# A loop over jobs of two matmul stages: the order of twelve matmuls, and the next expert's scales and first weight piece in branches

## The chip, the core and the metric

The kernel runs on one core of a Trainium2 chip. The metric is the device time of one execution in microseconds, lower is better. The engines of a core run side by side, each in the order of its own program: TensorE (PE, with its weight loads as PEld), VectorE (DVE), ScalarE (ACT), GpSimd (POOL) and SyncE (SP), which issues most DMAs. They wait for one another through semaphores.

## What is computed

An RWKV-like attention over 4 x 768 tokens gives rows of 384 numbers; each row then goes through one of eight experts. The change touches the experts alone. Of the reference:

```python
def _moe_ref(x, modality_id, w_gate, modality_bias, w1, w2):   # x: 3072 x 384, E = 8, F = 1024
    ...
    for e in range(E):
        mask = e_idx == e
        ...
        h = np.maximum(x[mask] @ w1[e], 0.0)
        out[mask] = gate_w[mask, None] * (h @ w2[e])
```

## The kernel before

Attention and routing fill about the first 200 us; there the tokens are written to `rows` in memory, sorted by expert, and nine tiles of 128 tokens of the fullest expert are worked on beside the attention. What is left is a table of jobs, made on the chip: each job is 128 tokens of one expert, and a job's code (a number) says what has to be done about weights beside it. The first job stands ahead of the loop (`up("a", ...)`, `job_terms`), the others are the turns of `tc.For_i` in `run`; in this run the loop makes 16 turns.

A matrix product in float32 is made of three float16 products. Weights `raw` are split into a high part `whi` (`wide`, ScalarE: scaled and rounded) and a low part `wlo` (`fine`, VectorE: what the rounding left), in six pieces: 0 to 2 are the first matrix, 3 to 5 the second. The scale `ws` comes from the sums of squares of `raw` (`norm`, ScalarE, into `ssq`), summed over partitions by a small matmul `pw` with ones on TensorE and turned into a power of two by four small VectorE operations (`scales_`). Tokens `xT` have both parts too.

One job on TensorE:

- `up`: the first matrix, in groups of 4, 2 and 2 blocks of 128 hidden units (`raise_`, 36, 18 and 18 matmuls of 128 columns). After each group ScalarE takes the relu's high part `hh` (`relu_high`) and VectorE its low part `hl` (`relu_low`). `beside()` after a group runs other work: behind group 0 `change(code, 5)` and `due`, behind group 1 `scales("2")`.
- `job_terms`: the second matrix, 20 of its 24 matmuls of 384 columns into `po`; a term is `hh` or `hl` of one block f with `whi` or `wlo`. Its order before: `hh whi` 0-3, `hh wlo` 0-3, `hh whi` 4-7, `hl whi` 0-3, `hh wlo` 4-7.
- `rest_terms`: `hl whi` 4-7, at the start of the next turn. Then `put`: ScalarE multiplies `po` by the tokens' factor `fac`, and POOL stores the rows by an indirect DMA at `ids`.

Around it in a turn: SP fetches the next job's tokens (`turn`, into `xn` and `mn`); VectorE copies them into `xT` and `m2` when `up` has read them (`take_in`). `due` makes `fac` and `ids` of the job from `m2`. Where the code says so, blocks of `tc.If` are entered: `square` (the next expert's sums of squares, two pieces a bit), `first_half` (the job ahead of a change of expert: pieces 0 to 2 are split into `whi` and `wlo` after the job's own use of them), `change` (the first job of a new expert: pieces 3, 4 and 5) and `next_load` (SP: the load of the weights after those). ScalarE and VectorE meet such a block in each job; where it isn't entered they compare, jump, and bring their semaphore to the count that the block would have left, for which they first wait for their own last operation.

The order of instructions inside a turn is that of the code (`manual_schedule`) on DVE, ACT, PE and SP.

Of the kernel before, what the change touches and what calls it, by code (L numbers as in the profile page):

```python
# [18 lines left out]
P = 128  # L19
# [18 lines left out]
NQ = 6  # L38
# [26 lines left out]
class _Kernel:  # L65
# [942 lines left out]
    def up(self, key, beside=lambda: None, late=False):  # L1008
        sizes = [4, 2, 2]
        for g, fb in enumerate(sizes):  # L1010
            f0 = sum(sizes[:g])
            ph = self.ps_a.tile([P, 512], F32, tag="big", name=f"ph{key}{g}")
            self.raise_(ph, f0, fb)
            self.relu_high(ph, f0, fb)
            low = lambda ph=ph, f0=f0, fb=fb: self.relu_low(ph, f0, fb)
            low()
            beside()

# [54 lines left out]
    def job_terms(self, po):  # L1073

        half = FB // 2
        for lo in (0, half):
            for f in range(lo, lo + half):
                self.term(po, 0, self.hh, self.whi, f, first=f == 0)
            if lo:
                for f in range(half):  # L1080
                    self.term(po, 0, self.hl, self.whi, f)
            for f in range(lo, lo + half):
                self.term(po, 0, self.hh, self.wlo, f)

    def rest_terms(self, po):
        for f in range(FB // 2, FB):
# [12 lines left out]
    def run(self):  # L1099
        nc, tc, m = self.nc, self.tc, self.m  # L1100
# [307 lines left out]
        xn = m.tile([P, 2 * DC, P], F16, name="xn", bufs=1)  # L1408
        mn = m.tile([P, 2, 4], I16, name="mn", bufs=1)
        self.turn(0, self.at(ROW, slice(1, 2), E * CAP, SP), mn, xn)  # L1410
        take_in = lambda: (nc.vector.tensor_copy(self.xT[:, :, :P], xn), nc.vector.tensor_copy(m2[:, 0, :], mn[:, 0, :]))
        take_in()
        po = self.ps_y.tile([P, 512], F32, tag="y", name="po")
        self.job_terms(po)
# [6 lines left out]
        def square(code):  # L1421
            with tc.If(code % (1 << pairs) > 0):
                for n in range(pairs):
                    with tc.If(code % (2 << n) >= 1 << n):
                        norms(2 * n, 2 * n + 1)

        def first_half(code):
            with tc.If(code % (2 << pairs) >= 1 << pairs):  # L1428
                for q in range(NQ // 2):
                    self.split(q, 2 if q == 0 else 1)  # L1430

        def change(code, q):
            with tc.If(code >= 1 << STEPS):  # L1433
                self.split(q)
                if q == NQ // 2:
                    self.undo()

        def next_load():
            more = self.at(MORE, i, 2 * E - 1, SP)
# [3 lines left out]
        with tc.For_i(1, nj, 1, iteration_sync="reg_based") as i, tc.manual_schedule(engines={getattr(mybir.EngineType, e) for e in MS[:4]}):  # L1443
# [4 lines left out]
            square(code)  # L1448
            self.put(po, 0, "b")
            change(code, 4)  # L1450
            beside = iter([lambda: (change(code, 5), self.due(m2)), lambda: self.scales("2")])
            self.up("b", lambda: next(beside, lambda: None)(), True)
            next_load()
            take_in()
            self.job_terms(po)
            first_half(code)
        self.rest_terms(po)
# [44 lines left out]
```

## Time and profile before

| | us |
|---|---|
| median of 3 runs | 353.18 |
| lowest and highest | 351.89, 359.52 |
| the profiled execution | 351.33 |
| its span, first to last instruction | 349.4 |

| engine | busy us | share of the span | instructions |
|---|---|---|---|
| PE | 328.5 | 94% | 5555 |
| PEld | 265.8 | 76% | 5555 |
| DVE | 221.4 | 63% | 740 |
| ACT | 179.1 | 51% | 476 |
| POOL | 156.6 | 45% | 230 |

The granted TensorE clock is 0.989 of full over the span. The loop's turns begin at 210.12 us and end near 342.4; the rest of the span behind it is the last job's rest and its store. Busy shares over the whole span say little of the loop, so the rows below are taken from its stretches. In a timeline, matmuls that follow each other in one group are merged into one row with their count, and the number of the row is from the first's start to the last's modelled end; where a wait lies inside such a row it is longer than its like.

### The profile page before, as it was taken

The numbers are of one execution on the slowest core, as the hardware profiler recorded it, in microseconds if no ns is written. First come the engines' busy times: TensorE is split into PE (matmuls) and PEld (weight loads), VectorE is DVE, ScalarE is ACT, GpSimd is POOL, SyncE is SP. The second block draws the span as 40 slices with busy tenths as digits, with TensorE's granted clock in tenths as the row PEclk, the third lists the DMA queues.
The fourth block names the chain that finished last, engine by engine and source line by source line (L and its number), as shares of the span: only waits on it lengthen the run. The fifth ranks groups of instructions, "written<-read, shape, count | busy, mean of one in ns | idle before, by whom it ended". The sixth has DMA issues, their size and how long they took to land. (4 is left out here: it accounts for less than half of the span.)

```text
span 349.4 us, 15387 instructions
## 1 busy us (share of the span) xinstructions
PE 328.5 (94%) x5555; PEld 265.8 (76%) x5555; DVE 221.4 (63%) x740; ACT 179.1 (51%) x476; POOL 156.6 (45%) x230
## 2 busy tenths in 40 slices
PE   8999998868999999999998999998999999999992
PEld 3788997757878888897887777776777777777771
DVE  8878899798997877684768633368333332333950
ACT  7777874966866748556532222265222224542920
POOL 8988869765737856242268311113112110221311
PEclk9999999989999999999999999999999999999997
DMA  6785868996649999492336531226821121112120
GB/s 190 222 166 159 179 164 253 328 257 146 162 114 212 244 290 216 99 197 72 70 115 202 170 103 35 58 50 220 192 67 45 45 62 29 45 45 68 23 58 5
DMA packets 56798, 46.96 MB, mean 134 GB/s; under 512 B 42920, under 2 KB 50359, under 8 KB 56496
## 3 DMA queue, kind: packets, MB, share of 16 engines
q1 hardware_dynamic: 53552, 36.86, 44.5%
q0 software_dynamic: 3200, 9.47, 7.7%
q8 instruction: 31, 0.51, 0.6%
q14 instruction: 15, 0.12, 0.1%
HBM read 26.03 MB, written 11.83 MB: 108 GB/s over the span
## 5 line engine op out<-in xcount | busy, mean ns | idle before, releaser
L997 PEld LDWEIGHTS <-whi 128*128 128x128 f16 x1248 | 72.4, 98 | 3.9 <-issue 1.1
L1006 DVE SCALAR_TENSOR_TENSOR hl<-phb,hh 128x256 f16<-128x256 f32 (+1 forms) x48 | 24.6, 512 | 69.3 <-ACTq L1433 47.8
L1060 PEld LDWEIGHTS <-hh 128*128 128x128 f16 x416 | 37.9, 98 | 31.9 <-ACTq L1428 3.8
L997 PE MATMUL phb<-mxT,whi 128*128 128x128 f16 x768 | 50.8, 219 | 0.0
L410 ACT ACTIVATE dv<-kv,d 128x48 f32<-128x48 f32 x172 | 43.0, 324 | 3.0 <-issue 2.0
L1001 ACT ACTIVATE hh<-phb 128x256 f16<-128x256 f32 (+1 forms) x48 | 21.4, 454 | 40.7 <-PE phb L997 21.4
L997 PEld LDWEIGHTS <-wlo 128*128 128x128 f16 x624 | 37.7, 98 | 0.2 <-DVE wlo L943 0.2
L371 POOL TENSOR_TENSOR rk<-rc,kc 112x512 f32<-112x512 f32 x20 | 25.7, 1286 | 24.1 <-DVE ebx L309 10.9
L966 POOL TENSOR_TENSOR seenb<-otb,putb 128x1 int32<-128x1 int32 x16 | 4.5, 282 | 64.8 <-ACTq L1433 51.6
L430 DVE TENSOR_TENSOR at<-psc,mask 128x512 f32<-128x512 f32 x48 | 31.7, 682 | 2.2 <-PE psc L424 2.1
L359 POOL TENSOR_TENSOR rc<-ud,powr 112x512 f32<-112x512 f32 (+1 forms) x25 | 31.2, 1252 | 2.7 <-DMA ud<-in_pd 1.9
L1060 PE MATMUL po<-whi,hh 128*128 128x384 f16 x136 | 29.7, 327 | 1.7 <-ACT whi L938 1.1
L1060 PEld LDWEIGHTS <-hl 128*128 128x128 f16 x208 | 19.5, 98 | 15.0 <-issue 3.0
L665 POOL DMA_INDIRECT rows<-row,posi x24 | 24.9, 1039 | 10.4 <-DVE pr L742 3.6
L1060 PE MATMUL po<-whi,hl 128*128 128x384 f16 x136 | 28.0, 326 | 1.5 <-DVE hl L1006 0.7
L997 PE MATMUL phb<-mxT,wlo 128*128 128x128 f16 x384 | 29.3, 219 | 0.0
L424 PE MATMUL psc<-rc,kc 64*64 64x128 f32 (+1 forms) x768 | 28.6, 286 | 0.6 <-issue 0.4
L1060 PE MATMUL po<-wlo,hh 128*128 128x384 f16 x136 | 27.7, 326 | 0.0
L957 ACT ACTIVATE otb<-po,fac 128x384 f32<-128x384 f32 x16 | 9.3, 579 | 35.6 <-PE phb L997 28.5
L997 PE MATMUL phs<-mxT,whi 128*128 128x128 f16 x432 | 27.2, 219 | 0.0
L424 PEld LDWEIGHTS psc<-rc,kc 64*64 64x64 f32 (+1 forms) x768 | 22.1, 138 | 6.5 <-issue 2.9
L943 DVE SCALAR_TENSOR_TENSOR wlo<-raw,ws,whi 128x1024 f16<-128x1024 f32 (+1 forms) x20 | 25.4, 1299 | 1.9 <-ACT whi L938 1.2
(272 smaller groups left out, 641.2 us busy)
## 6 DMA issues: line engine op xcount, KB each, us to landing
kv<-in_pt SPq DMA_DIRECT2D x21, 384.0 KB
raw<-in_w SPq DMA_DIRECT2D x12, 512.0 KB
ud<-in_pd SPq DMA_DIRECT2D x12, 384.0 KB
raw<-in_w SPq DMA_DIRECT2D x2, 1536.0 KB, 7.3
ud<-in_pd SPq DMA_DIRECT2D x12, 192.0 KB
rows<-pad SPq DMA_DIRECT2D x10, 193.0 KB
kv<-in_pt SPq DMA_DIRECT2D x6, 192.0 KB
rows<-row,posi POOLq DMA_INDIRECT x24
```

What stands on the lines that cost most here:

```text
L359: nc.gpsimd.tensor_mul(u["rc"][:TOP, s], u["rT"][:TOP, s], self.powr[:TOP, s])
L371: nc.gpsimd.tensor_mul(u["rk"][:TOP], u["rc"][:TOP], u["kc"][:TOP])
L410: nc.scalar.activation(u["dv"][:, sl], u["v"][:, sl], AF.Copy, scale=u["d"][:, h : h + 1])
L424: nc.tensor.matmul(u["ps"][j][s, pr * P : (pr + 1) * P], u["kc"][r, pr, s], u["rc"][r, pr, :], start=True, stop=True)
L430: nc.vector.tensor_mul(u["at"][:, j * NPR : (j + 1) * NPR, :], u["ps"][j].rearrange("p (q t) -> p q t", q=NPR), self.mask.unsqueeze(1).to_ ...
L665: i = nc.gpsimd.indirect_dma_start(out=self.rows, out_offset=bass.IndirectOffsetOnAxis(ap=u["posi"][:, b : b + 1], axis=0), in_=u["row"][: ...
L943: self.nc.vector.scalar_tensor_tensor(self.wlo[:, sl], self.raw[:, sl], sc, self.whi[:, sl], ALU.mult, ALU.subtract)
L957: self.nc.scalar.activation(ot, po[:, :DM], AF.Copy, scale=gf[:, t : t + 1])
L997: self.nc.tensor.matmul(ph[:, q * P : (q + 1) * P], w[:, c0 : c0 + P], self.xT[:, xq, t * P : (t + 1) * P], start=i == q == 0, stop=i == l ...
L1001: self.nc.scalar.activation(self.hh[:, f0 : f0 + fb, t * P : (t + 1) * P], p3, AF.Relu)
L1006: self.nc.vector.scalar_tensor_tensor(self.hl[:, f0 : f0 + fb, r], p3, 0.0, self.hh[:, f0 : f0 + fb, r], ALU.max, ALU.subtract)
L1060: self.nc.tensor.matmul(po[:, :DM], h[:, f, t * P : (t + 1) * P], w[:, c0 : c0 + DM], start=first, stop=last)
```

## The change

Four things, all in the table's jobs:

- `job_terms` takes `hl whi` 0-3 ahead of `hh whi` 4-7.
- The scales are no longer made in each job behind group 1. The small matmul `pw` stands behind group 0 of each job, and the four VectorE operations are in a branch that is entered only in the job ahead of a change (`weigh`), together with the two halves of `wide` for piece 0. This stands ahead of `relu_low` of group 0.
- Behind `relu_low` of group 0 comes `either`: a branch for the jobs of a change or ahead of one, holding `change(code, 5)` and, in a further branch, the two halves of `fine` for piece 0. `first_half` keeps pieces 1 and 2.
- `due` moves from behind group 0 to `take_in`, between its two copies.

```diff
@@ -1013,6 +1013,8 @@
             self.raise_(ph, f0, fb)
             self.relu_high(ph, f0, fb)
             low = lambda ph=ph, f0=f0, fb=fb: self.relu_low(ph, f0, fb)
+            if late and g == 0:
+                beside()
             low()
             beside()
 
@@ -1074,13 +1076,9 @@
 
         half = FB // 2
         for lo in (0, half):
-            for f in range(lo, lo + half):
-                self.term(po, 0, self.hh, self.whi, f, first=f == 0)
-            if lo:
-                for f in range(half):
-                    self.term(po, 0, self.hl, self.whi, f)
-            for f in range(lo, lo + half):
-                self.term(po, 0, self.hh, self.wlo, f)
+            for h, w in ((self.hh, self.whi), (self.hh, self.wlo), (self.hl, self.whi))[: 2 if lo else 3]:
+                for f in range(lo, lo + half):
+                    self.term(po, 0, h, w, f, first=f == 0 and h is self.hh and w is self.whi)
 
     def rest_terms(self, po):
         for f in range(FB // 2, FB):
@@ -1408,7 +1406,7 @@
         xn = m.tile([P, 2 * DC, P], F16, name="xn", bufs=1)
         mn = m.tile([P, 2, 4], I16, name="mn", bufs=1)
         self.turn(0, self.at(ROW, slice(1, 2), E * CAP, SP), mn, xn)
-        take_in = lambda: (nc.vector.tensor_copy(self.xT[:, :, :P], xn), nc.vector.tensor_copy(m2[:, 0, :], mn[:, 0, :]))
+        take_in = lambda between=lambda: None: (nc.vector.tensor_copy(self.xT[:, :, :P], xn), between(), nc.vector.tensor_copy(m2[:, 0, :], mn[:, 0, :]))
         take_in()
         po = self.ps_y.tile([P, 512], F32, tag="y", name="po")
         self.job_terms(po)
@@ -1424,16 +1422,34 @@
                     with tc.If(code % (2 << n) >= 1 << n):
                         norms(2 * n, 2 * n + 1)
 
+        near = lambda code: tc.If(code % (2 << pairs) >= 1 << pairs)
+
         def first_half(code):
-            with tc.If(code % (2 << pairs) >= 1 << pairs):
-                for q in range(NQ // 2):
-                    self.split(q, 2 if q == 0 else 1)
+            with near(code):
+                for q in range(1, NQ // 2):
+                    self.split(q)
 
         def change(code, q):
             with tc.If(code >= 1 << STEPS):
                 self.split(q)
                 if q == NQ // 2:
                     self.undo()
+
+        def weigh(code):
+            steps = self.scales_("2")
+            next(steps)
+            with near(code):
+                for _ in steps:
+                    pass
+                for part in range(2):
+                    self.wide(0, part, 2)
+
+        def either(code):
+            with tc.If(code >= 1 << pairs):
+                change(code, NQ - 1)
+                with near(code):
+                    for part in range(2):
+                        self.fine(0, part, 2)
 
         def next_load():
             more = self.at(MORE, i, 2 * E - 1, SP)
@@ -1448,10 +1464,10 @@
             square(code)
             self.put(po, 0, "b")
             change(code, 4)
-            beside = iter([lambda: (change(code, 5), self.due(m2)), lambda: self.scales("2")])
+            beside = iter([lambda: weigh(code), lambda: either(code)])
             self.up("b", lambda: next(beside, lambda: None)(), True)
             next_load()
-            take_in()
+            take_in(lambda: self.due(m2))
             self.job_terms(po)
             first_half(code)
         self.rest_terms(po)
```

The first place is on TensorE, between the first and the second half of `job_terms` in a turn of the loop. Before (`REGISTER_ALU` works out the count that is waited for):

```order
L1060 LDWEIGHTS hh
L1060 MATMUL po<-wlo,hh 128x384
L1060 REGISTER_ALU
L1060 LDWEIGHTS hh [waits Activation_I-4853_own]
L1060 MATMUL po<-whi,hh 128x384
L1060 LDWEIGHTS hh
L1060 MATMUL po<-whi,hh 128x384
```

and before, further down, where `hl` 0-3 began:

```order
L1060 LDWEIGHTS hh
L1060 MATMUL po<-whi,hh 128x384
L1060 REGISTER_ALU
L1060 LDWEIGHTS hl [waits DVE_I-4853_own]
L1060 MATMUL po<-whi,hl 128x384
L1060 LDWEIGHTS hl
L1060 MATMUL po<-whi,hl 128x384
```

Now:

```order
L1062 LDWEIGHTS hh
L1062 MATMUL po<-wlo,hh 128x384
L1062 REGISTER_ALU
L1062 LDWEIGHTS hl [waits DVE_I-4853_own]
L1062 MATMUL po<-whi,hl 128x384
```

and, behind the last `hl` term of that half:

```order
L1062 LDWEIGHTS hl
L1062 MATMUL po<-whi,hl 128x384
L1062 REGISTER_ALU
L1062 LDWEIGHTS hh [waits Activation_I-4853_own]
L1062 MATMUL po<-whi,hh 128x384
```

The weight load that waits for ScalarE's `hh` 4 has moved four terms down, and the one that waits for VectorE's `hl` 0 four terms up.

The second place is on TensorE too: the small matmul `pw` (it reads `wssq`, the sums of squares, and waits for ScalarE). Before it stood between group 1 (`phb_4966`) and group 2 (`phb_4995`):

```order
L997 LDWEIGHTS wlo
L997 MATMUL phb_4966<-mxT,wlo 128x128
L922 REGISTER_ALU
L922 LDWEIGHTS onesb [waits Activation_I-4853_own]
L922 MATMUL pw_4987<-wssq,onesb 128x6 [waits PE_49]
L997 LDWEIGHTS whi
L997 MATMUL phb_4995<-mxT,whi 128x128 [waits PE_49]
```

Now it stands between group 0 (`phb_4922`) and group 1 (`phb_4987`):

```order
L997 LDWEIGHTS wlo
L997 MATMUL phb_4922<-mxT,wlo 128x128
L922 REGISTER_ALU
L922 LDWEIGHTS onesb [waits Activation_I-4853_own]
L922 MATMUL pw_4960<-wssq,onesb 128x6 [waits PE_49]
L997 LDWEIGHTS whi
L997 MATMUL phb_4987<-mxT,whi 128x128
```

Two groups instead of one are queued behind that wait.

The third place is on VectorE, around the low part `hl` of group 0. Before, it stood directly behind the block of `change(code, 4)` (L1433), and was followed by the block of `change(code, 5)`:

```order
L1433 REGISTER_ALU
L1433 UNCONDITIONAL_BRANCH [waits DVE_I-4853_own]
L1006 ISA
L1006 SCALAR_TENSOR_TENSOR hl<-phb_4922,hh 128x4x128 [waits DVE_I-4853_own,Activation_I-4853_own,PE_49]
L1433 COMPARE_AND_BRANCH
L943 REGISTER_ALU
L943 SCALAR_TENSOR_TENSOR wlo<-raw,ws,whi 128x1024 [waits DMAHW3_I-4853_own,Activation_I-4853_own,PE_49]
```

Now the branch of `weigh` (L1441, its last rows are shown) stands ahead of it, and it is followed by `either` (L1448):

```order
L311 TENSOR_SCALAR ws<-ebw_4969 128x2 [waits DVE_I-4853_own,Activation_I-4853_own,DVE_49]
L314 TENSOR_SCALAR winv<-ebw_4969 128x2 [waits DVE_49]
L1441 UNCONDITIONAL_BRANCH
L1441 REGISTER_ALU
L1441 UNCONDITIONAL_BRANCH [waits DVE_I-4853_own]
L1006 ISA
L1006 SCALAR_TENSOR_TENSOR hl<-phb_4922,hh 128x4x128 [waits DVE_I-4853_own,Activation_I-4853_own,PE_49]
L1448 COMPARE_AND_BRANCH
L1433 COMPARE_AND_BRANCH
```

The row of group 0's `hl` has a block before it and the outer test of `either` behind it. ScalarE passes the same two blocks between its `hh` of group 0 and of group 1.

## Rows read from the trace of the kernel before

**Rows 1.** Busy times by stretch: start and end, length, each engine's busy us.

```profile
core 0: us, PE busy (x) PEld busy (x) DVE busy (x) ACT busy (x) POOL busy (x), PEclk, DMA share, GB/s
210.12:226.29 16.17, 16.14 (x196) 12.62 (x194) 5.28 (x22) 3.89 (x8) 2.72 (x6) 1.00 0.14 37
226.29:243.70 17.41, 16.46 (x196) 12.51 (x194) 12.59 (x30) 10.07 (x15) 4.35 (x5) 1.00 0.47 135
243.70:251.91 8.21, 8.21 (x99) 6.25 (x99) 2.80 (x11) 1.94 (x4) 1.36 (x3) 1.00 0.95 223
251.91:284.47 32.56, 32.51 (x389) 25.28 (x389) 10.59 (x45) 7.77 (x16) 5.62 (x13) 1.00 0.20 49
284.47:317.36 32.89, 32.45 (x390) 25.41 (x388) 10.01 (x44) 14.42 (x28) 5.44 (x12) 1.00 0.19 48
317.36:334.74 17.38, 16.42 (x196) 12.49 (x194) 12.59 (x30) 10.07 (x15) 4.52 (x6) 1.00 0.18 41
```

**Rows 2.** Timeline of job 2: start, us, instruction, [idle before, what ended it].

```profile
221.28 0.69 DVE L1006 SCALAR_TENSOR_TENSOR hl<-phb,hh 128x512 f16<-128x512 f32 x1 [4.67 <-ACTq L1433]
...
222.19 0.81 PE L1060 MATMUL po<-whi,hh 128*128 128x384 f16 x4
...
222.43 0.38 ACT L1001 ACTIVATE hh<-phb 128x256 f16<-128x256 f32 x1 [1.25 <-PE L1060]
...
223.49 1.02 PE L1060 MATMUL po<-whi,hh 128*128 128x384 f16 x4
223.57 0.38 ACT L1001 ACTIVATE hh<-phb 128x256 f16<-128x256 f32 x1 [0.76 <-PE L1060]
...
224.01 0.11 PEld L1060 LDWEIGHTS <-hh 128*128 128x128 f16 x2 [0.42 <-ACTq L1428]
```

**Rows 3.** Timeline of TensorE in job 16, second half of `job_terms`.

```profile
340.12 0.97 PE L1060 MATMUL po<-whi,hh 128*128 128x384 f16 x4
```

**Rows 4.** Timeline of TensorE in job 4, the first change.

```profile
239.22 0.82 PE L1060 MATMUL po<-whi,hh 128*128 128x384 f16 x4 [0.53 <-ACT whi L938]
...
243.38 0.48 PE L1060 MATMUL po<-whi,hl 128*128 128x384 f16 x2 [0.36 <-DVE hl L1006]
```

**Rows 5.** Timeline of TensorE in jobs 11, 12 and 13.

```profile
297.23 0.82 PE L1060 MATMUL po<-whi,hh 128*128 128x384 f16 x4 [0.41 <-ACTq L1433]
...
303.15 0.83 PE L997 MATMUL phb<-mxT,whi 128*128 128x128 f16 x12
...
311.24 0.83 PE L997 MATMUL phb<-mxT,whi 128*128 128x128 f16 x12
```

**Rows 6.** Timeline of ScalarE in the same jobs: ends of squares, a relu.

```profile
294.29 0.19 ACT L907 ACTIVATION_READ_ACCUMULATOR junk<-raw 128x1 f32 x1
...
297.57 0.70 ACT L1001 ACTIVATE hh<-phb 128x256 f16<-128x256 f32 x2 [0.40 <-ACTq L1433]
...
302.87 0.19 ACT L907 ACTIVATION_READ_ACCUMULATOR junk<-raw 128x1 f32 x1
...
311.42 0.19 ACT L907 ACTIVATION_READ_ACCUMULATOR junk<-raw 128x1 f32 x1
```

**Rows 7.** Timeline of VectorE in jobs 3 and 4.

```profile
232.88 1.41 DVE L943 SCALAR_TENSOR_TENSOR wlo<-raw,ws,whi 128x512 f16<-128x512 f32 x2
...
239.97 0.68 DVE L1006 SCALAR_TENSOR_TENSOR hl<-phb,hh 128x512 f16<-128x512 f32 x1
...
242.27 0.16 DVE L925 TENSOR_REDUCE wtot<-pw 128x2 f32<-128x6 f32 x1
...
242.81 0.42 DVE L1006 SCALAR_TENSOR_TENSOR hl<-phb,hh 128x256 f16<-128x256 f32 x1
```

**Rows 8.** Timeline of ScalarE from the end of job 3.

```profile
232.13 4.46 ACT L938 ACTIVATE whi<-raw,ws 128x512 f16<-128x512 f32 x5
```

**Rows 9.** Timeline at the end of job 5, all engines.

```profile
251.40 0.36 DVE L1411 COPY mxT<-xn 128x768 f16<-128x768 f16 x1 [1.48 <-DMA xn<-rows]
```

**Rows 10.** Timeline behind the loop's end, all engines.

```profile
343.12 0.81 PE L1060 MATMUL po<-whi,hl 128*128 128x384 f16 x4 [0.73 <-PEq L1498]
```

## The prediction

> **What bounds the kernel now.** I read the busy times of stretches first, because the change touches only the loop over the table's jobs [rows 1]. I count its turns as jobs 1 to 16; the weights change in jobs 4 and 15. TensorE is busy almost without a break there (16.14 of 16.17 us in jobs 1 and 2) at full clock, so what a job could lose is its length beyond its matmuls. The timeline of job 2 [rows 2] gives that floor: the first down-term starts at 222.19, 4.05 us after the job's start at 218.14, and eight terms later it is 223.49, so four terms take 0.65; 4.05 + 6 x 0.65 = 7.95 us. Against n x 7.95 the stretches of [rows 1] have an excess of 0.27 (jobs 1, 2), 1.51 (3, 4), 0.26 (5), 0.76 (6 to 9), 1.09 (10 to 13) and 1.48 us (14, 15), together 5.37 of 124.62. With 0.16 in job 16 (a row of 0.97 where 0.81 is normal, [rows 3]) that is 5.5 us or 1.6% of the profiled execution's 351.33: all that the change can win, since it removes no matmul but its reading of waits.
>
> Where the excess sits: in a plain job at the third and fourth `hh` term of the second half, a merged row of 1.02 us at 223.49 where 0.81 is normal; the row at 224.01 names the weight load that waited. The high part of group 2 ran only from 223.57 to 223.95, because ScalarE, idle 1.25 and 0.76 us before groups 1 and 2, is released late [rows 2]. In a change job there are two waits, for ScalarE's weights and group 0's high part (239.22) and for VectorE's last low part (243.38) [rows 4]. In jobs 11 and 12 TensorE waits for ScalarE (297.23), which takes the next expert's squares first [rows 5, 6].
>
> **The change, part by part.** *`hl` 0-3 ahead of `whi` 4-7.* Same matmuls, other order. `hl` of group 0 is ready at 221.28 + 0.69 = 221.97 and would be read at 223.49; `hh` 6 and 7 are then wanted 0.65 later, about 224.5, ready at 223.95 [rows 2]. So the wait of plain jobs goes: -0.27 in jobs 1 and 2, -0.70 in jobs 6 to 9 (0.76 less 0.06 behind a late transfer), -0.16 in job 16.
>
> *Scale sums in a branch.* Four small VectorE operations leave 14 of 16 jobs: 0.54 us by 242.27 to 242.81 [rows 7]. I cost it at nothing: VectorE is busy 5.28 of 16.17 us [rows 1]; without that cover it would be a gain of 0.54 a job.
>
> *`fac` and `ids` later.* Two operations of about 0.3 us now stand between the copies of `xT` and `mt`; the copy of `xT`, which TensorE needs, keeps its place. ScalarE wants `fac`, and POOL `ids`, only in the next job. Nothing, with the same cover.
>
> *More blocks.* ScalarE and VectorE pass two blocks instead of one between group 0 and group 1. One block not entered leaves ScalarE 0.40 us idle (297.57, one of three such rows, [rows 6]), while the two relus behind it run back to back. I take 0.30 for the second block (between nothing and 0.40). In a plain job it hides in the 1.25 us that ScalarE idles there anyway [rows 2]. In jobs 11 to 13 it doesn't: there ScalarE's own order sets the time. The Trainium skill, "Runtime: NRT & Kernel Launch", section "Instruction fetch mechanics", speaks against such blocks: a jump to code outside the two pages that an engine holds forces a fetch before it goes on. The 0.40 across a block that is already there does not look like that, and the new jumps are as short. By the row the sum is the one below; by the page each block could be a stall, whose outcome is the second rival.
>
> *`pw` behind group 0.* TensorE's small matmul for the scales waits for the squares (ScalarE), and groups 1 and 2 now queue behind it. In the 13 jobs without squares, the squares are long done: nothing. Job 11: the squares end at 294.48, about when group 0 ends; TensorE waits anyway until 297.23 [rows 5, 6]. Job 12: group 0 ends at 303.15, the squares at 303.06; job 13: 311.24 against 311.61 [rows 5, 6]. Now job 10's gain is lost, since job 11 is bound by ScalarE. The second block delays ScalarE by 0.30 in job 11 (0.08 comes back where a test is shared), so job 12's squares end near 303.2 and TensorE's first down-term comes 0.15 late; again 0.22 later job 13's squares end near 311.98. TensorE, back at its floor, is at `pw` at about 311.4 and waits 0.7 us; its first down-term is 0.85 later than before. Less the 0.17 that job 13 loses today: jobs 10 to 13 cost **+0.7**. From below: no delay and no wait there, -0.35 (the two plain waits); from above: two blocks at 0.73 (second rival), +3.0.
>
> *Piece 0 and the scales in jobs 3 and 14, ahead of a change.* ScalarE's run of five multiplications (4.46 us at 232.13 [rows 8]) becomes two early and three late, so in job 4 group 0's high part is no longer what TensorE waits for. VectorE is: from 232.88 to 243.23 it has hardly a gap [rows 7]. The low parts of piece 0 (1.41) leave that run, but they now stand ahead of the low parts of groups 1 and 2 and of the copy of `xT` in job 3, which come some 0.75 later, and `fac`, `ids` 0.35 ahead of piece 1. In job 4 `fac`, `ids` and the scale sums go (0.9), and two blocks not entered come in, in front of the low parts of groups 0 and 1, where VectorE first waits for its own last operation (0.25 each, an estimate from the 0.40), with 0.4 of block entries in job 3. Sum: -1.41 + 0.75 + 0.35 - 0.9 + 0.5 + 0.4 = -0.3. And the stall changes its place: `hl` 0-3 is wanted 1.3 us after the first down-term, but group 0's low part still comes behind pieces 3 and 4, ending at 240.65 today [rows 7]. So TensorE will wait about 1 us at the first `hl` term. I take -0.2 for each pair; ends: nothing, and -1.5, the pair's whole excess.
>
> *Job 5.* The tokens of job 6 arrive behind the weight load: VectorE waited 1.48 us for them and copied at 251.40 [rows 9], with the DMA engines 0.95 busy [rows 1]. The load starts when VectorE has finished the old weights, so what jobs 3 to 5 win is mostly lost here: jobs 3 to 5 together -0.1 instead of -0.36.
>
> Sum: -0.27 - 0.1 - 0.70 + 0.7 - 0.2 - 0.16 = **-0.7 us**. Against the profiled execution's 351.33 that is 350.6. It lies 1.85 below the median of the runs (353.18, from 351.89 to 359.52), so I forecast 352.4.
>
> **Rivals.** *All waits go.* If VectorE's run in the change jobs shortens by piece 0's 1.41 with nothing given back, and the squares are not waited for, the plain waits (2.0 in 12 jobs) and half to all of the change jobs' go: -2.5 to -4.5, say 347.8 here, 349.6 in runs. For it: the work that leaves really stood on the last wait (243.38, [rows 4]). Against it: `hl` is wanted earlier.
>
> *Blocks cost more (slower).* Place: ScalarE in jobs 11 to 13, between group 0 and group 1. The only long wait at a jump in the loop's rows is 0.73 us, as TensorE leaves the loop [rows 10]. At 0.73 a block the two add 1.2 us per job beyond what I counted; job 12 and job 13 inherit it through the squares, and jobs 10 to 13 cost about +3.0: in all +1.6, 352.9 here, 354.8 in runs. It turns the sign where a job's extra delay passes 0.6. Against it: the 0.40 across a block [rows 6].
>
> *The move does nothing.* TensorE's late release may come from something that follows the order, so that the stall reappears at the next `hh` term; then jobs 1 to 9 win nothing and +0.2 to +0.7 is left: 351.8 here, 353.7 in runs. Against it: `hh` 6 is done 0.5 us before its new place.
>
> **How the numbers follow.** Forecast 0.55, all waits go 0.17, dearer blocks 0.16, nothing moved 0.12. The likeliest gives 352.4, alone from 351.4 to 353.6 (its parts' bounds, with the runs' level). The range 349.2 to 355.0 takes in the middle of both outer cases. A difference under 2%, about 7 us, is what a measurement of this kernel can hardly tell from no change; since the excess is 5.5 us in all, a gain beyond it would need something outside the loop (0.02), and a loss beyond it several new waits in every job (0.03): within 0.95.
>
> **What would show it.** Right: plain jobs of 7.95 to 8.0 us with no weight load waiting at the second half; in job 13 a gap of some 0.7 before `pw`; in jobs 4 and 15 no wait at the first down-term but one near 1 us at the first `hl` term. Wrong: `hh` waits that stay; relus of groups 1 and 2 later than 1.4 us after the first down-term in plain jobs; job 13 no longer than 8.0; change jobs under 8.6.

## The result, and the profile after

The changed kernel is not faster. Its median is 355.18 us (22 runs, 352.81 to 358.82); the kernel before, run 22 times beside it, has 355.15 (349.88 to 359.52). Compared without the runs in a slower state, which are taken to be those more than 1.5% above the kernel's own fastest (half of before's, two of the changed kernel's), the ratio is 1.0074, with an interval from 1.0049 to 1.0099: about 2.6 us slower. Since the medians over all runs are equal, the size of the loss is read below from the loop of the profiled executions, stretch by stretch. The forecast was 352.4, 0.7 us less than before. The level that it was given at, the median of three runs, was itself 2 us lower than that of the 22.

The profiled execution of after takes 357.0 us (span 355.0, granted clock 0.981), 5.67 more than that of before. Its loop starts at 212.46 instead of 210.12. These 2.34 us are not the change's: ahead of the loop only the first job has a new order, and it takes 7.95 us in after and 7.94 in before. From the start of job 1 to that of job 16 it lasts 128.44 us, where it was 124.62: **+3.82 in the loop**. The busy times of the same stretches as in [rows 1], with the same columns (start and end, length, busy us of each engine, granted clock, DMA share, GB/s):

```profile
212.46:228.34 15.88, 15.88 (x195) 12.78 (x194) 4.32 (x14) 3.89 (x8) 2.72 (x6) 1.00 0.14 37
228.34:245.80 17.46, 16.42 (x197) 12.52 (x195) 12.16 (x25) 10.12 (x15) 4.58 (x5) 1.00 0.24 47
245.80:256.09 10.29, 8.11 (x98) 6.29 (x97) 2.13 (x7) 1.95 (x4) 1.36 (x3) 1.00 0.86 326
256.09:289.51 33.42, 33.42 (x388) 27.21 (x389) 8.93 (x31) 7.79 (x16) 5.63 (x13) 0.95 0.19 47
289.51:323.44 33.93, 32.61 (x390) 25.59 (x388) 8.45 (x28) 14.35 (x28) 5.45 (x12) 1.00 0.20 47
323.44:340.90 17.46, 16.42 (x197) 12.51 (x194) 12.18 (x25) 10.12 (x15) 4.58 (x5) 1.00 0.17 40
```

Against [rows 1]: jobs 1 and 2 -0.29, jobs 3 and 4 +0.05, job 5 **+2.08**, jobs 6 to 9 **+0.86** at a lower clock, jobs 10 to 13 **+1.04**, jobs 14 and 15 +0.08. Three places hold the loss.

*The load of the next weights.* The timeline of SP in job 4, first of before, where the row's duration runs from the first issue to the end of the second:

```profile
237.15 5.14 SPq L904 DMA_DIRECT2D raw<-in_w  x2
```

Then the timeline of after, jobs 4 to 6, SP, VectorE and TensorE:

```profile
244.11 0.98 SPq L904 DMA_DIRECT2D raw<-in_w  x2
...
255.67 0.36 DVE L1409 COPY mxT<-xn 128x768 f16<-128x768 f16 x1 [3.71 <-DMA xn<-rows]
...
256.09 2.57 PE L997 MATMUL phb<-mxT,whi 128*128 128x128 f16 x24 [2.19 <-DVE mxT L1409]
258.45 1.45 PE L997 MATMUL phb<-mxT,wlo 128*128 128x128 f16 x12
```

Before, the first half was asked for 2.7 us into job 4 (which starts at 234.48), while VectorE still had some 5 us of the old weights' low parts to do; the second followed near 242. Now both halves go out together, 7.8 us into job 4 (which starts at 236.29), 0.2 us after VectorE has ended piece 5's low part (242.63 + 1.28, next timeline). The tokens of job 6, behind them, arrive so late that VectorE waits 3.71 us for them (1.48 in [rows 9]) and TensorE 2.19. What follows runs at the lower of the two clock levels (1.2 and 2.4 GHz; the granted clock of the stretch is 0.95): 24 matmuls take 2.57 us and 12 take 1.45, in place of 1.50 and 0.83 elsewhere. Job 6 lasts 9.59 us; jobs 7 to 9 last 7.95 each.

*The change jobs.* The timeline of job 4, VectorE, ScalarE and TensorE:

```profile
241.38 1.15 ACT L938 ACTIVATE whi<-raw,ws 128x1024 f16<-128x1024 f32 x1 [1.37 <-DVEq L1441]
...
241.48 0.69 DVE L1006 SCALAR_TENSOR_TENSOR hl<-phb,hh 128x512 f16<-128x512 f32 x1 [0.35 <-DVEq L1441]
242.63 1.28 DVE L943 SCALAR_TENSOR_TENSOR wlo<-raw,ws,whi 128x1024 f16<-128x1024 f32 x1 [0.46 <-ACT whi L938]
244.56 0.76 DVE L1006 SCALAR_TENSOR_TENSOR hl<-phb,hh 128x256 f16<-128x256 f32 x2 [0.65 <-ACTq L1433]
...
242.23 0.82 PE L1062 MATMUL po<-whi,hl 128*128 128x384 f16 x4 [0.43 <-DVE hl L1006]
...
245.13 0.82 PE L1062 MATMUL po<-whi,hl 128*128 128x384 f16 x4 [0.52 <-DVE hl L1006]
```

The wait at the first down-term [rows 4] is gone. There is one at the first `hl` term, as the prediction said, and the one at the last `hl` terms has grown (0.52 us, 0.36 in [rows 4]). ScalarE was idle for 1.37 us ahead of piece 5, until VectorE had passed `weigh` (L1441), and VectorE's last low part then waited 0.46 for piece 5. Job 4 itself lasts 9.51 us instead of 9.22; the pair shows only +0.05 because job 3 has lost its wait in the down-terms and takes 7.95 instead of 8.19.

*The jobs with squares.* TensorE's `pw` and ScalarE's relu of group 1 in jobs 11 to 13, from their timelines:

```profile
300.16 0.18 PE L922 MATMUL pw<-wssq,onesb 128*128 128x6 bf16 x1 [0.53 <-ACTq L1422]
...
308.62 0.18 PE L922 MATMUL pw<-wssq,onesb 128*128 128x6 bf16 x1 [0.18 <-ACTq L1422]
...
317.50 0.18 PE L922 MATMUL pw<-wssq,onesb 128*128 128x6 bf16 x1 [0.61 <-ACT junk L907]
...
303.07 0.66 ACT L1001 ACTIVATE hh<-phb 128x256 f16<-128x256 f32 x2 [0.77 <-PE po L1062]
```

All three jobs wait at `pw`, and ScalarE is idle 0.77 us ahead of group 1's relu, where it was 0.40 with one block [rows 6].

### The profile page after: what moved, and what is told of

The parts are those of the page before. It is cut to its first block, busy times and chain, and to the rows that moved or that the text cites. A ratio compares the mean times of both kernels' runs of the same rounds, so it can differ in the third digit from the quotient of the medians.

```text
span 355.0 us, 15411 instructions
## 1 busy us (share of the span) xinstructions
PE 330.5 (93%) x5555; PEld 270.0 (76%) x5555; DVE 215.0 (61%) x684; ACT 179.4 (51%) x476; POOL 158.4 (45%) x230
## 3 DMA queue, kind: packets, MB, share of 16 engines
q0 software_dynamic: 3200, 9.47, 7.4%
## 5 line engine op out<-in xcount | busy, mean ns | idle before, releaser
L997 PEld LDWEIGHTS <-whi 128*128 128x128 f16 x1248 | 74.3, 99 | 6.0 <-DVE mxT L1409 2.6
L1062 PEld LDWEIGHTS <-hh 128*128 128x128 f16 x416 | 38.8, 98 | 27.6 <-ACT hh L1001 2.0
L997 PE MATMUL phb<-mxT,whi 128*128 128x128 f16 x768 | 51.7, 221 | 2.2 <-DVE mxT L1409 2.2
L997 PEld LDWEIGHTS <-wlo 128*128 128x128 f16 x624 | 39.0, 100 | 0.0
L359 POOL TENSOR_TENSOR rc<-ud,powr 112x512 f32<-112x512 f32 (+1 forms) x25 | 32.2, 1291 | 3.6 <-DMA ud<-in_pd 2.7
L965 POOL TENSOR_TENSOR putb<-ids,none 128x1 int32<-128x1 int32 x16 | 2.9, 180 | 63.1 <-DVE mt L1409 60.5
L997 PE MATMUL phs<-mxT,whi 128*128 128x128 f16 x432 | 28.2, 224 | 0.0
L1062 PE MATMUL po<-whi,hh 128*128 128x384 f16 x136 | 27.7, 326 | 0.0
L461 PE MATMUL py<-kv,at 128*64 128x48 f32 x768 | 26.7, 222 | 0.0
```

The source lines that it names most:

```text
L359: nc.gpsimd.tensor_mul(u["rc"][:TOP, s], u["rT"][:TOP, s], self.powr[:TOP, s])
L461: nc.tensor.matmul(py[t, sl], u["at"][:, j * NPR + pr, t], u["v"][:, sl], start=c == h == 0, stop=h == H - 1, skip_group_check=True)
L997: self.nc.tensor.matmul(ph[:, q * P : (q + 1) * P], w[:, c0 : c0 + P], self.xT[:, xq, t * P : (t + 1) * P], start=i == q == 0, stop=i == l ...
L1062: self.nc.tensor.matmul(po[:, :DM], h[:, f, t * P : (t + 1) * P], w[:, c0 : c0 + DM], start=first, stop=last)
```

## Experiments

"The loop" is the time from the start of job 1 to that of job 16 in the profiled execution. Ratios are to the kernel before on the same chip. The late load, the two kernels behind it and the first run of the order alone ran on one chip (the first), all others on a second one, where the median of before is some 5 us higher. Which chip the result above was taken on isn't recorded.

**Is a late load enough?** The kernel before, its halves asked for in the other order:

```diff
-                self.load(more % E, 2, 0, 1)
+                self.load(more % E, 2, 1, 0)
```

> The kernel before with the two halves of the weight load asked for in the other order (pieces 3 to 5 first), so that both wait for the last low part of piece 5 near 241.9 us; nothing else differs. Theory: a load that starts 4.8 us later is enough for the loss of the changed kernel. It takes some 11 us (10.9 in the changed kernel), so that the tokens of job 6 come near 253.5 instead of 251.4: jobs 5 and 6 together 2 us longer, and 3.5 to 4 us if TensorE, idle for that long, comes back at half clock as in the changed kernel: a ratio of 1.006 to 1.011. Rival: the load is hidden, or its order is of no account; then the ratio is 1.000 and job 5 stays 8.2.

Ratio 1.0049 (1.0012 to 1.0086). Timeline of SP, VectorE and TensorE in jobs 4 to 6, and the stretches of jobs 5 and 6:

```profile
240.37 0.93 SPq L904 DMA_DIRECT2D raw<-in_w  x2
...
252.37 2.72 PE L997 MATMUL phb<-mxT,whi 128*128 128x128 f16 x24 [2.17 <-DVE mt L1411]
...
242.09:252.37 10.28, 8.12 (x98) 6.33 (x98) 2.54 (x11) 2.53 (x5) 1.61 (x4) 0.99 0.87 329
252.37:261.87 9.50, 9.50 (x98) 7.95 (x98) 2.45 (x11) 1.36 (x3) 1.17 (x2) 0.83 0.25 53
```

With nothing else changed, the load 7.2 us into job 4 (which starts at 233.18) gives the changed kernel's two long jobs, 10.28 and 9.50 us, half clock included: 3.9 us more than twice 7.95. A late load is enough. The ratio is a little under the expected 1.006 to 1.011, which its interval overlaps.

**What made it late?** The changed kernel with piece 0 split where it was before:

```diff
-                for q in range(1, NQ // 2):
-                    self.split(q)
+                for q in range(NQ // 2):
+                    self.split(q, 2 if q == 0 else 1)
...
-                for part in range(2):
-                    self.wide(0, part, 2)
...
-            with tc.If(code >= 1 << pairs):
-                change(code, NQ - 1)
-                with near(code):
-                    for part in range(2):
-                        self.fine(0, part, 2)
+            change(code, NQ - 1)
```

> The changed kernel with piece 0 of the next weights split where it was before (behind the down-terms of the job ahead of a change, in front of pieces 1 and 2); the scales stay behind group 0. Theory: the load of the next weights waited because the last reader of its first half had moved into a block behind the last piece; with that reader back, the first half is asked for near 237 us on the clock of the kernel before (2.7 us into job 4, instead of 7.8), job 5 lasts 8.0 to 8.3 us instead of 10.29, and job 6 7.95 instead of 9.58 with all its matmuls at full clock. Jobs 10 to 13 keep 33.9. In all 3 to 4 us faster than the changed kernel, a ratio to before of 0.995 to 0.998. Rival: the late tokens come from elsewhere (the copy with the factors between, the blocks on VectorE); then job 5 stays above 9.5 and the ratio near 1.007.

The changed kernel with the first half's load written ahead of the blocks:

```diff
             square(code)
+            next_load(0)
...
-            next_load()
+            next_load(1)
```

> The changed kernel with the first half of the weight load written ahead of the blocks of the same turn (behind the squares), the second half where it was. Theory (SP waits at the join of a block that is not entered): the first half then waits only for the low parts of the turn before and goes out by about 237 us or earlier, 4.5 us or more ahead of the changed kernel's; job 5 lasts 8.0 to 8.3 us, job 6 7.95, jobs 3 and 4 stay at 17.4 to 17.6 and jobs 10 to 13 at 33.9: 3.3 to 3.9 us faster than the changed kernel, a ratio to before near 0.997. Rival: the load's start follows VectorE's work as such (it isn't the block); then the first half still goes out behind the last low part, job 5 stays near 10.3 and the ratio near 1.007.

Ratios 0.9989 (0.9945 to 1.0032) and 1.0024 (0.999 to 1.0058). SP's issue and the stretch of job 5, of the first:

```profile
234.77 5.86 SPq L904 DMA_DIRECT2D raw<-in_w  x2
...
241.54:249.49 7.95, 7.95 (x100) 6.39 (x98) 2.19 (x7) 1.95 (x4) 1.54 (x4) 1.00 0.69 234
```

and of the second:

```profile
234.21 5.63 SPq L904 DMA_DIRECT2D raw<-in_w  x2
...
241.25:249.19 7.94, 7.94 (x98) 6.39 (x97) 2.24 (x8) 1.95 (x4) 1.54 (x4) 1.00 0.68 228
```

In both, the first half goes out 2.3 to 2.5 us into job 4, and jobs 5 and 6 last 7.94 to 7.95. Both ratios lie above what was expected (0.995 to 0.998, and near 0.997), the first with an interval that covers it; a likely reason is that this chip doesn't give the order's gain (below). The second kernel moves nothing but the place of the first half's load in the program, so the work of piece 0 isn't what held it: it was the block. `fine` of piece 0, in `either` behind the low part of piece 5, is the last reader of that half in program order. In job 4 it isn't executed, but SP has to wait until VectorE has passed it.

**Do the waits that the order removes belong to the kernel?** In the three kernels above plain jobs last 7.95, in the one with the old order too. So the order alone was run, on both chips, and on the second the two kernels themselves:

```diff
-            for f in range(lo, lo + half):
-                self.term(po, 0, self.hh, self.whi, f, first=f == 0)
-            if lo:
...
+            for h, w in ((self.hh, self.whi), (self.hh, self.wlo), (self.hl, self.whi))[: 2 if lo else 3]:
+                for f in range(lo, lo + half):
```

> The kernel before with one part of the change, the new order of the down-terms, and nothing else. Theory: the order alone ends the hh waits of the plain jobs, and the load of the next weights starts as early as before, since nothing else moved. Then every plain job of the loop lasts 7.95 us (jobs 1 and 2 15.9 instead of 16.17, jobs 6 to 9 31.8 to 31.9 instead of 32.56, job 5 about 8.1), jobs 10 to 13 32.5 instead of 32.89 (ScalarE's squares stay), jobs 3 and 4 17.2 to 17.5: in all 1.5 to 2.2 us faster than before, a ratio near 0.995. Rival 1: the plain waits went in the changed kernel because the scale sums left VectorE and the blocks moved; then the waits of 0.2 us stay here and the ratio is 1.000. Rival 2: the loss of the changed kernel comes from the order itself (hl is wanted earlier); then this kernel is slower, 1.005 or more.

> The kernel before, unchanged, profiled beside the others of this call. Theory: the waits at the third and fourth hh term of the plain jobs depend on the chip. In the profile that the prediction read, TensorE's counts reach ScalarE late while POOL's indirect transfer is issued (the relu of group 1 starts 1.85 us after that of group 0); in the four kernels profiled on another chip it starts 1.0 to 1.2 us after, with the old order of the terms too. So: on a chip with late counts plain jobs last 8.0 to 8.2 us here, on one without 7.95, with the relu of group 1 about 1.16 us behind that of group 0, and jobs 1 to 16 are 1.5 to 2 us shorter than in the first profile (133.6 us up to the last rest term). Rival: the waits belong to the kernel (old order, old blocks), and it was the moved load or the new order that ended them in those four; then plain jobs last 8.05 to 8.2 here on any chip.

> The changed kernel, unchanged, profiled on the same chip as the kernel before. Theory: its losses are of its own order and show on any chip: job 5 10.2 to 10.4 us, job 6 9.5 to 9.6 (half clock behind the idle time), jobs 11 to 13 26.0 against 24.1 to 24.4, change jobs 9.5 against 8.9 to 9.2. On a chip without late counts the order wins nothing, so the loop is 5.5 to 6.5 us longer than before's (ratio 1.012 to 1.018); on one with late counts 3.5 to 4.5 us longer (1.008 to 1.012). Rival: the loss is one of the chip of the first comparison (its DMA engines, its clock); then on another chip the load is asked for early or job 5 stays near 8.2 and the ratio is within 1.003.

> Once more the kernel before with the new order of the down-terms alone, for a chip whose counts from TensorE come late (told by the relu of group 1, 1.65 us or more behind that of group 0 in plain jobs; 1.16 on the chip of the first run, where the order won nothing). Theory: on a chip with late counts the order wins what the prediction gave it: plain jobs 7.95 instead of 8.0 to 8.2, the loop 1.6 to 2.3 us shorter, ratio 0.993 to 0.996; on one without, 0.997 to 1.002 again. Rival: late counts make the hl terms wait as well, since they are wanted 0.65 us earlier; then plain jobs stay above 8.0 there and the ratio is 1.000.

On the first chip the order alone gives a ratio of 0.9995 (0.9959 to 1.003) where 0.995 was expected, on the second **0.9932** (0.99 to 0.9963). The stretches of jobs 1 and 2 and of jobs 6 to 9, of the order alone on the second chip:

```profile
211.70:227.59 15.89, 15.89 (x196) 12.79 (x194) 5.28 (x22) 3.89 (x8) 2.72 (x6) 1.00 0.14 37
...
253.59:285.48 31.89, 31.89 (x389) 25.61 (x389) 10.52 (x45) 7.77 (x16) 5.62 (x13) 1.00 0.20 49
```

and of the kernel before there (its span of 359.0 us and its granted clock of 0.961 come from stretches outside the loop; in the loop the clock is 1.00):

```profile
219.41:235.61 16.20, 16.16 (x196) 12.62 (x194) 5.28 (x22) 3.89 (x8) 2.73 (x6) 1.00 0.14 37
...
261.34:293.97 32.63, 32.48 (x390) 25.24 (x388) 10.56 (x44) 7.79 (x16) 5.46 (x12) 1.00 0.20 49
```

Jobs 1, 2 and 6 to 9 win 1.05 us, but the whole loop only 0.99 (123.93 against 124.92), less than the 1.6 to 2.3 that were expected: what jobs 3 and 10 win comes back in jobs 4 and 11 (9.47 against 9.23, 8.85 against 8.54), which wait for VectorE's and ScalarE's work on the weights. Why the runs show more than the profiled loop, 0.7%, is open.

The difference between the chips is in ScalarE's release. Timeline of ScalarE, the relu of group 1 in job 2, with the old order: before on the second chip,

```profile
231.75 0.38 ACT L1001 ACTIVATE hh<-phb 128x256 f16<-128x256 f32 x1 [1.26 <-PE L1060]
```

and the kernel with the late load on the first:

```profile
220.89 0.38 ACT L1001 ACTIVATE hh<-phb 128x256 f16<-128x256 f32 x1 [0.56 <-PE phb L997]
```

ScalarE learns 0.7 us later on the second chip (as in [rows 2]) that the same matmuls are done. It is so in nearly all plain jobs of the kernels profiled there, but for the one below, and in none on the first chip, with the old order or the new. The waits in plain jobs hang on that; on the first chip there is nothing to win by the order.

The changed kernel on the second chip repeats its pattern: job 5 10.14, job 6 9.57, jobs 11 to 13 25.99 (before there: 8.33, 8.16, 24.76), loop 128.28 against 124.92, +3.36. Yet its runs give a ratio of only 1.0021 (0.9992 to 1.0051), less than was expected. So on this chip the runs show no clear loss. Why they lose less than the profiled loops is open; one thing that can differ from run to run is the clock of job 6 (below).

**Who delays the counts?** The kernel before without the loop's stores:

```diff
-            self.put(po, 0, "b")
+            self.put(po, 0, "b", send=False)
```

> The kernel before without the indirect transfers of the loop: POOL computes the rows' places but sends no row, so the rows of the loop's jobs but the last are missing from the output. Theory: on a chip with late counts it is POOL's indirect transfer, issued while group 1 runs, that holds TensorE's counts back; without it the relu of group 1 comes 1.0 to 1.2 us behind that of group 0 and plain jobs last 7.95 us instead of 8.0 to 8.2, with the old order. Rival: the counts are late by themselves there; then 1.65 to 1.85 us and 8.0 to 8.2 stay. On a chip without late counts it changes nothing and tells nothing.

Timeline of ScalarE in job 2, and the stretch of jobs 6 to 9:

```profile
229.97 0.38 ACT L1003 ACTIVATE hh<-phb 128x256 f16<-128x256 f32 x1 [0.56 <-PE phb L999]
...
259.12:290.90 31.78, 31.78 (x390) 25.57 (x388) 9.79 (x44) 7.78 (x16) 1.51 (x8) 1.00 0.15 28
```

On the second chip, with the old order, the late release is gone and plain jobs last 7.95. The loop is 121.13 us, 3.8 less than before's there. It is POOL's indirect transfer that holds the counts back. In before's job 2 it is issued around the start of group 1 (its timeline):

```profile
220.06 0.99 POOL L967 DMA_INDIRECT out<-otb,putb  x1 [0.56 <-issue]
```

The trace of before also records when TensorE's semaphore steps: the steps come some 0.03 us apart, but stand still for 0.59 us from 220.03 and for 0.68 from 220.68. In job 2 of the kernel with the late load, on the first chip, the longest pause beside the same transfer is 0.09 us. Whether it is the transfer's issue or its data that does it, no run separates.

**Squares: the wait at `pw`, or ScalarE's second block?** The changed kernel with `pw` at the end of the turn before:

```diff
-            steps = self.scales_("2")
-            next(steps)
...
             self.job_terms(po)
+            next(self.scales_("3", pt=pt))
```

> The changed kernel with one part undone: TensorE's small matmul for the scales no longer stands behind group 0 but at the end of the turn before, so nothing waits for the squares there; ScalarE's two blocks stay. Theory A (ScalarE's second block is the cost): jobs 11 to 13 keep most of their loss, 25.0 to 25.6 us instead of 26.0, with the wait now at the first down-term (relu of group 0). Theory B, the prediction's (the wait for the squares in front of that matmul is the cost): jobs 11 to 13 go back to 24.1 to 24.8. In both jobs 5 and 6 stay at 10.3 and 9.6 and the ratio to before is 1.000 to 1.008.

Ratio 1.0012 (0.9991 to 1.0033). The stretch of jobs 11 to 13, and TensorE's start of job 6:

```profile
295.64:321.20 25.56, 24.36 (x293) 19.18 (x292) 6.21 (x21) 12.13 (x24) 4.09 (x9) 1.00 0.20 47
...
255.90 1.51 PE L998 MATMUL phb<-mxT,whi 128*128 128x128 f16 x24 [2.06 <-DVE mxT L1410]
```

25.56 lies where theory A put it. Of the 1.23 us that jobs 11 to 13 lost on this chip (25.99 less 24.76), 0.43 go with the wait at `pw` and 0.80 stay with the second block: jobs 11 and 12 are 0.34 and 0.42 longer than before's, job 13 0.04. The first chip gives the same split. The stretches of jobs 11 to 13 there, of the late load (old order, one block), of piece 0 back (`pw` behind group 0, but again one block on ScalarE, idle 0.39 ahead of group 1's relu) and of the early half (`pw` behind group 0, two blocks, idle 0.77):

```profile
293.65:317.74 24.09, 24.09 (x294) 19.19 (x291) 7.33 (x33) 11.55 (x24) 4.08 (x9) 1.00 0.18 46
...
289.21:313.67 24.46, 24.20 (x293) 19.19 (x291) 6.30 (x21) 11.40 (x24) 4.08 (x9) 1.00 0.20 50
...
288.92:314.18 25.26, 24.47 (x292) 19.19 (x291) 6.23 (x21) 11.43 (x24) 4.08 (x9) 1.00 0.20 49
```

The wait at `pw` alone costs 0.37, the second block 0.80 more. Both expectations had jobs 10 to 13 at 33.9 us; they came to 32.41 and 33.21, the first because taking piece 0 back also took away ScalarE's second block.

In the kernel with `pw` at the end of the turn, the second row was not expected: TensorE idled 2.06 us here too, but came back at full clock, so that job 6 lasts 7.96 and not 9.6.

**The change jobs, and the price of a block.** The changed kernel with piece 5 in a block ahead of the one with the scales:

```diff
+        def last_high(code):
+            with tc.If(code >= 1 << STEPS):
+                self.wide(NQ - 1)
...
-            beside = iter([lambda: weigh(code), lambda: either(code)])
+            beside = iter([lambda: (last_high(code), weigh(code)), lambda: either(code)])
```

> The changed kernel with piece 5's multiplication on ScalarE in a block of its own ahead of the block with the scales (its low part on VectorE stays where it was). Theory: in the change jobs ScalarE waited 0.86 us there because that block may write the scales on VectorE, which passes it only behind its own last low part; ahead of it the multiplication needs no wait, the last low part of piece 5 no longer waits 0.46 us, and jobs 4 and 15 last 9.0 to 9.2 us instead of 9.51 (0.3 to 0.5 less each); the weight load, still behind that low part, goes out some 0.4 us earlier, which job 5 wins too. All else as in the changed kernel: about 1.2 us faster than it. Rival: VectorE's queue sets the change jobs by its work alone; then they stay at 9.5.

Ratio 1.0054 (1.001 to 1.0098). Timeline of ScalarE and VectorE in job 4, then ScalarE in job 11, and the stretches of job 15 and of jobs 11 to 13:

```profile
238.82 1.14 ACT L938 ACTIVATE whi<-raw,ws 128x1024 f16<-128x1024 f32 x1
...
241.51 1.27 DVE L943 SCALAR_TENSOR_TENSOR wlo<-raw,ws,whi 128x1024 f16<-128x1024 f32 x1
...
302.43 0.66 ACT L1001 ACTIVATE hh<-phb 128x256 f16<-128x256 f32 x2 [1.11 <-PE po L1062]
...
331.09:340.18 9.09, 8.31 (x99) 6.20 (x97) 8.08 (x12) 4.73 (x7) 2.17 (x3) 1.00 0.14 34
296.42:323.15 26.73, 24.67 (x293) 19.20 (x292) 6.30 (x21) 12.23 (x24) 4.08 (x9) 1.00 0.18 45
```

Piece 5 no longer waits, nor does VectorE for it; job 4 takes 9.32 (9.0 to 9.2 expected) and job 15 9.09 instead of 9.51. For job 15 this mend may not be the cause: with `pw` at the end of the turn, where piece 5 still waited, it took 9.14. The gain is lost again (loop 128.66 against 128.28, where 1.2 us less was expected): a third block costs ScalarE 0.34 us more in front of group 1 and jobs 11 to 13 another 0.74, which the expectation left out. Job 5 won nothing (10.37).

All mends together (early half, piece 5 ahead, `pw` at the end of the turn), and then the same with ScalarE's work between groups 0 and 1 in one outer block:

```diff
+            with tc.If(code >= 1 << pairs):
+                with tc.If(code >= 1 << STEPS):
+                    self.wide(NQ - 1)
+                with near(code):
```

> The changed kernel with three mends: the first half of the weight load ahead of the blocks, piece 5's multiplication ahead of the block with the scales, and TensorE's small matmul for the scales at the end of the turn, behind the down-terms, instead of behind group 0 (its tile is filled once ahead of the loop). Theory: each loss has its own cause, so each mend acts in its own stretch: job 5 8.0 and job 6 7.95 (load), jobs 4 and 15 9.0 to 9.2 (block), jobs 11 to 13 24.0 to 24.6 instead of 26.0 with no wait in front of that matmul (squares). The loop is then 5 to 6 us shorter than the changed kernel's, as long as before's on a chip without late counts (ratio 0.997 to 1.002), 1 to 2 us shorter on one with them (0.995). Rival: without the wait for the squares the delay comes back as a wait for ScalarE's relus behind them, so that jobs 11 to 13 stay above 25.

> The changed kernel with the early first half of the load, TensorE's small matmul at the end of the turn, and everything that ScalarE does between the relus of groups 0 and 1 in one outer block (piece 5's multiplication, then the scales and piece 0, each in a block inside it), so that ScalarE passes one block there instead of two or three. Theory: jobs 11 to 13 are set by ScalarE, and a block that is not entered costs it 0.34 to 0.37 us each time (idle before the relu of group 1: 0.40 with one block, 0.77 with two, 1.11 with three). So 0.40 here, and jobs 11 to 13 take 24.1 to 24.8 us together instead of 26.0 (two blocks) or 26.2 (three, without the wait for the squares). Jobs 5 and 6 8.0, change jobs 8.9 to 9.3, plain jobs 7.95: ratio to before 0.987 to 0.992 with late counts, 0.997 to 1.000 without. Rival: what costs there is the wait for the squares or the work of piece 0; then jobs 11 to 13 stay above 25.5.

Ratios 0.995 (0.9917 to 0.9984) and 0.9963 (0.9919 to 1.0006). The stretches of jobs 11 to 13 and ScalarE's relu of group 1 in job 11, with three blocks and no wait at `pw`:

```profile
296.97 0.66 ACT L1002 ACTIVATE hh<-phb 128x256 f16<-128x256 f32 x2 [1.11 <-PE po L1063]
...
291.01:317.22 26.21, 24.37 (x294) 19.18 (x292) 6.20 (x21) 12.09 (x24) 4.09 (x9) 1.00 0.19 45
```

and with the one outer block:

```profile
299.88 0.72 ACT L1002 ACTIVATE hh<-phb 128x256 f16<-128x256 f32 x2 [0.61 <-PE po L1063]
...
294.36:319.77 25.41, 24.33 (x293) 19.17 (x291) 6.20 (x21) 12.31 (x24) 4.09 (x9) 1.00 0.20 48
```

The first kernel's load mend held (jobs 5 and 6: 7.94 and 7.95; jobs 4 and 15: 9.22 and 9.25), and its loop is 4.2 us shorter than the changed kernel's (5 to 6 expected), but its jobs 11 to 13 did not come back to 24.0 to 24.6: the rival held, the delay moved to the relus. The second missed as well, by less, in these jobs and in its ratio (0.987 to 0.992 expected): with one outer block that holds two others ScalarE idles 0.61 us, not 0.40, and its jobs 4 and 15 grew to 9.88 and 9.64, for a reason that stays open. The first of the two is faster than before by its interval, the second isn't shown to be. Neither is shown to beat the order alone, which has 0.9932 on the second chip and no difference on the first.

## Why the prediction was wrong

**The step that failed is "Job 5".** It says: "The load starts when VectorE has finished the old weights". Half of the load never did: in before it goes out at 237.15, and VectorE is at the old weights until shortly before 242.27 [rows 7]. From that sentence followed that no edit could make the load later than it was, so the step only asked how much of a gain it would swallow. It should have asked, for each half of `raw`, which instruction is its last reader in program order, before and after; that one moved from `first_half` of job 3 to behind piece 5 in job 4. The two stretches that hold it (job 5 and jobs 6 to 9) were predicted at about 0 and -0.70 and came out at +2.08 and +0.86. The difference is idle time of TensorE (2.19 us) and the clock behind it (1.64, by which job 6 is longer than 7.95). Without these two stretches' 2.08 and 1.64 the sum is +0.1 instead of +3.82: no loss, but no gain either. The rest of the way from the prediction's -0.57 for these stretches lies in jobs 10 to 13 and in the change jobs (below).

Part of the miss in microseconds is the level and no mechanism: the median of three that the forecast started from was 2 us under that of the 22, out of the 2.8 between 352.4 and 355.18.

**Plain jobs: right, on a chip with late counts.** Jobs 1 and 2 gave -0.29 (predicted -0.27), each plain job 7.95, and job 16's long row is normal again. ScalarE is released late in after too (1.31 us idle ahead of group 1's relu in job 2); the order only wants its result later, as the prediction said. What the prediction took for a property of the kernel is one of the chip: on the first chip of the experiments the same edit is worth nothing. The trace couldn't show that; the odd releaser in [rows 2], a matmul that follows those waited for, might have warned.

**Jobs 10 to 13: right mechanism, wrong shares.** Predicted +0.7, measured +1.04. `pw` waits in job 13 as said (0.61 us idle, predicted 0.7), but also in 11 and 12 (0.53 and 0.18), where no wait of its own was counted. ScalarE's second block measures 0.77 - 0.40 = 0.37, not 0.30 less 0.08. And most of the loss is that block, not the wait: 0.80 against 0.43 on one chip, 0.80 against 0.37 on the other. The rival "blocks cost more" gave 354.8 us in runs, next to the 355.18 measured, but that is luck: its price of 0.73 a block did not come. The page "Runtime: NRT & Kernel Launch" of the Trainium skill, section "Instruction fetch mechanics", has a fetch stall for jumps out of reach. No run here shows whether such a fetch is in the 0.34 to 0.37 us of each further small block, or in the 0.61 of the nested one.

**Change jobs: +0.05 and +0.08 for the pairs instead of -0.2.** The wait did move from the first down-term to the first `hl` term (0.43 us idle, about 1 expected). Not seen was that `weigh` may write `ws`, which ScalarE's piece 5 reads: a block that isn't entered made ScalarE wait for VectorE, and VectorE in turn for ScalarE. Taking that apart gave 0.19 us in job 4; what of job 15's 0.42 is due to it is open.

## What to carry to other kernels

A block that is not entered still stands in the program: whoever waits for the last reader or writer of a buffer waits until its engine has passed that block, so before moving work into a branch, list each buffer it touches with the transfers and engines that wait for it, and write those ahead of the block. A transfer that starts early is a gain that no busy time shows; read when each load is issued, not only when it lands. And a gain that is read from waits of 0.2 us in one profile may belong to that chip: where an engine is released by something behind what it waits for, a second chip's profile decides.

## What the runs showed that was not expected

- TensorE's release of ScalarE is 0.7 us late on one chip while POOL's indirect transfer is issued (idle 1.26 before the relu of group 1), and not late on another (0.56); without the transfer it is not late on the former either (0.56).
- After about 2 us without work TensorE ran many of the next matmuls at the lower clock level in four profiled executions (2.19 us idle in after, 2.03 in after on the second chip, 2.17 with the late load, 2.27 with piece 5 ahead) and at full clock in one (2.06, `pw` at the end of the turn). The length of the idle time doesn't decide it, since 2.03 lost the clock and 2.06 kept it; what does is open.
- A block that isn't entered costs ScalarE 0.34 to 0.37 us in a row of them (0.40, 0.77, 1.11 us idle for one, two, three); with one that holds two others it idles 0.61.
